# Attention with a sliding window and a GEGLU block: reciprocals through a DRAM tile, q and k by halves, scores half a batch ahead

## The chip, the core and the metric

The kernel runs on one core of a Trainium2 chip. Time is the device time of one execution in microseconds (us). One execution of the kernel before was also profiled; its span is counted from the first to the last recorded event. The engines are called TensorE (PE), VectorE (DVE), ScalarE (ACT), GpSimd (POOL) and SyncE (SP). PEld is TensorE's load of weights; SPq and POOLq are the instruction queues of SyncE and GpSimd, which here issue transfers (DMAs).

## The reference

Eight batches, eight heads, 576 positions, 64 values per head. Each query sees itself and the 127 positions before it, with a bias that falls off linearly with the distance. The heads side by side make rows of 512, 4608 of them, which go through a gated block of width 1536.

```python
scores = scale * np.matmul(q, k.transpose(0, 1, 3, 2))
rel = pos[:, None] - pos[None, :]
mask = (rel >= 0) & (rel < window)
scores = np.where(mask, scores + bias[None], -1000000000.0)
attn = np.exp(scores - max)
attn = attn / (np.sum(attn, axis=-1, keepdims=True) + 1e-09)
x = np.matmul(attn, v)            # to (4608, 512)
out = (gelu(x @ w_gate) * (x @ w_val)) @ w_out
```

## The kernel before

**Attention, batch by batch.** GpSimd loads q and k of a batch (`load_qk`, L75) in slabs of 128 positions by all eight heads and turns them into bf16 on the way: five transfers for q, five for k, the last of 64 positions. There is one slab buffer for q and one for k. The first batch is transposed by TensorE (`transposes`, L110); every other one by SyncE with transposing transfers (`transposes_dma`, L123), five for k and then five for q, each from 128 (or 64) positions by 512 columns into `kT` and `qT`, of which there are two sets, for even and odd batches.

The scores of a batch are eight steps (`scores`, L303): for each pair of heads c the blocks j = 1, 2 (`scores1`), then j = 0, 3 (`scores2`); block 4 of two pairs is done with the first of them (`scores0`). A step is a few matmuls of 64 rows (L135), the exponential on ScalarE (L142) into the tile `P`, and on VectorE the product with a mask that holds window and bias (L145). `P` has three buffers of two pairs each. `sums` (L189) adds up the weights with matmuls against ones, and VectorE takes the reciprocals (L203, L204). They stand in sixteen equal rows for each head and are spread over 64 partitions for each head by 32 copies on SyncE (L212) into the tile `rb`. `values` (L214) multiplies the weights with v for one pair and VectorE multiplies by `rb` (L227), which gives `xT`.

**The gated block, in nine groups of 512 rows.** `gate_val` (L233) makes one of twelve tiles of 128 hidden columns: eight matmuls (L240), gelu on ScalarE (L244), a product on VectorE (L245). `out_half` (L249) is half of one of four output tiles: six matmuls of 512 columns (L255); after the second half the tile is copied to `osb` (L261, or in the last groups L105 and L107 in turn) and SyncE stores it (L265).

**Order.** Each engine works through its instructions in the order of the program; SyncE and GpSimd also issue their transfers in that order, and one that waits holds all that stand behind it. PSUM has eight banks, taken in turn. Before the groups batches 0 and 1 are scored, with values(0) among the scores of batch 1. In group g the loads and transposes of batch g+2 are issued first, then come the twelve gate tiles with the four values of batch g+1 among them (after tiles 4, 6, 8 and 10), then the eight score steps of batch g+2 with an output half behind each of the first seven, then sums(g+2) and the last half. Groups 6 to 8 have no scores.

At the start GpSimd issues q and k of batch 0, makes the constants, and issues v of batch 0, q and k of batch 1, the weights in eight transfers (L97), v of batch 1 and the output weights (L301). The masks of all heads are made at once.

Of the kernel before, what the change touches and what calls it, by code (L numbers as in the profile page):

```python
# [7 lines left out]
FP32 = mybir.dt.float32  # L8
BF16 = mybir.dt.bfloat16
AF = mybir.ActivationFunctionType  # L10
# [14 lines left out]
def kernel(  # L25
# [10 lines left out]
    nc = tc.nc  # L36
# [21 lines left out]
    def bank():  # L58
        return psum.tile([128, 512], FP32, name="ps")
# [12 lines left out]

    slabs = {}

    def load_qk(b):  # L75
        for nm, src in (("qsb", q), ("ksb", k)):
            t = slab.tile([128, 5, DM], BF16, name=nm)
            slabs[nm, b] = t
            for j in range(5):
                sz = min(128, S - 128 * j)  # L80
                nc.gpsimd.dma_start(  # L81
                    out=t[0:sz, j, :].rearrange("p (h d) -> p h d", h=H),
                    in_=src[b][:, 128 * j:128 * j + sz, :].rearrange("h p d -> p h d"),
                )
# [16 lines left out]
    flip = [0]  # L101

    def evac(dst, src):
        if flip[0] % 2 == 0:
            nc.vector.tensor_copy(out=dst, in_=src)  # L105
        else:
            nc.scalar.copy(out=dst, in_=src)  # L107
        flip[0] += 1

    def transposes(b, i):  # L110
        nm, c = (("qsb", "ksb")[i // 4], i % 4)
        src = slabs[nm, b]
        ps = bank().bitcast(BF16)
        for j in range(5):
            sz = min(128, S - 128 * j)
            nc.tensor.transpose(  # L116
                out=ps[:, 128 * j:128 * j + sz],
                in_=src[0:sz, j, 128 * c:128 * (c + 1)],
                identity=ident[0:sz, 0:sz])
        dst = qT[b % 2][:, c, :] if nm == "qsb" else kT[b % 2][:, c, 64:64 + S]  # L120
        evac(dst, ps[:, 0:S])

    def transposes_dma(b):  # L123
        for nm, dst, off in (("ksb", kT[b % 2], 64), ("qsb", qT[b % 2], 0)):
            for j in range(5):
                sz = min(128, S - 128 * j)
                nc.sync.dma_start_transpose(  # L127
                    out=dst[:, :, off + 128 * j:off + 128 * j + sz],
                    in_=slabs[nm, b][0:sz, j, :])

    probs = {}

# [56 lines left out]
    def sums(b):  # L189

        ps = [bank(), bank()]
        for j in range(5):
            for s, a, e, col in pieces(j):
                for i in (0, 1):
                    for c in range(4):
                        nc.tensor.matmul(  # L196
                            out=ps[s][32 * c:32 * c + 32, a - QS * s:e - QS * s],
                            lhsT=ones[:, i, :],
                            rhs=probs[b, c - c % 2][:, c % 2, i, col:col + e - a],
                            start=(i == 0 and j == 2 * s), stop=(i == 1 and j == 2 * s + 2),  # L200
                            skip_group_check=True)
        r = r_pool.tile([128, S], FP32, name="r")
        nc.vector.reciprocal(r[:, 0:QS], ps[0][:, 0:QS])  # L203
        nc.vector.reciprocal(r[:, QS:S], ps[1][:, 0:S - QS])  # L204
        rb = r_pool.tile([128, 4, S], FP32, name="rb")
        recip[b] = rb
        for c in range(4):
            for i in (0, 1):
                row = 32 * c + 16 * i
                for m in range(4):  # L210
                    lo = 64 * i + 16 * m
                    nc.sync.dma_start(out=rb[lo:lo + 16, c, :], in_=r[row:row + 16, :])  # L212

    def values(b, c):  # L214
        P = probs[b, c - c % 2][:, c % 2]
# [33 lines left out]
    def out_half(g, u):  # L249
        t, half = u // 2, u % 2  # L250
        if half == 0:
            acc[g] = bank()
        po = acc[g]
        for f in range(6 * half, 6 * half + 6):
            nc.tensor.matmul(  # L255
                out=po, lhsT=hid[g][:, f, 128 * t:128 * (t + 1)],
                rhs=wo[:, f, :], start=(f == 0), stop=(f == NF - 1))
        if half == 1:
            osb = o_pool.tile([128, DM], FP32, name="osb")
            if g < B - 2:  # L260
                nc.vector.tensor_copy(out=osb, in_=po)  # L261
            else:
                evac(osb, po)
            r0 = 512 * g + 128 * t
            nc.sync.dma_start(out=out[r0:r0 + 128, :], in_=osb)  # L265


    load_qk(0)
    nc.vector.memset(ident, 0.0)
    nc.gpsimd.affine_select(  # L270
        out=ident, in_=ident, compare_op=ALU.not_equal, fill=1.0,
        base=0, pattern=[[-1, 128]], channel_multiplier=1)
    relt = consts.tile([128, 256], mybir.dt.int32, name="relt")
    tmpl = consts.tile([128, 256], FP32, name="tmpl")
    nc.gpsimd.iota(relt, pattern=[[1, 256]], base=0, channel_multiplier=-1)
    nc.gpsimd.tensor_copy(out=tmpl, in_=relt)
    for base, step, chan in ((0, 1, -1), (W - 1, -1, 1)):
        nc.gpsimd.affine_select(
            out=tmpl, in_=tmpl, compare_op=ALU.is_ge, fill=1e9,
            base=base, pattern=[[step, 256]], channel_multiplier=chan)  # L280
    load_v(0)
    for i in range(2):
# [6 lines left out]
    for h in range(H):  # L289
        slope = 2.0 ** (-8.0 * (h + 1) / H)  # L290
        nc.scalar.activation(out=emask[:, h, :], in_=tmpl, func=AF.Exp, scale=-slope)
    nc.vector.tensor_copy(out=emask2[:, :, 0:256], in_=emask)
    nc.vector.memset(emask2[0:64, :, 256:448], 0.0)
    nc.vector.tensor_copy(out=emask2[64:128, :, 256:448], in_=emask[64:128, :, 64:256])
    nc.vector.tensor_copy(out=emask2[:, :, 448:576], in_=emask[:, :, 0:128])
    step = DFF // 4
    load_qk(1)
    for s in range(4):
        load_w(step * s, step * (s + 1))
    load_v(1)  # L300
    nc.gpsimd.dma_start(out=wo, in_=moe_w_out.rearrange("(c p) f -> p c f", p=128))  # L301

    def scores(b):  # L303

        for c in range(4):
            if c % 2 == 0:
                yield lambda c=c: (scores0(b, c), scores1(b, c))
            else:
                yield lambda c=c: scores1(b, c)
            yield lambda c=c: scores2(b, c)  # L310


    for i in (0, 1, 2, 3):
        transposes(0, i)
        transposes(0, 4 + i)
    transposes_dma(1)
    for st in scores(0):
        st()
    sums(0)
    first = list(scores(1))  # L320
    for st in first[0:4]:
        st()
    for c in range(2):
        values(0, c)
    for st in first[4:8]:
        st()
    for c in range(2, 4):
        values(0, c)
    sums(1)

    for g in range(NG):
        if g + 2 < B:
            load_qk(g + 2)
            transposes_dma(g + 2)
        for f in range(NF):
            gate_val(g, f)
            if g + 1 < B and f in (4, 6, 8, 10):
                values(g + 1, f // 2 - 2)  # L340
        b = g + 2
        if b < B:
            load_v(b)
            for u, st in enumerate(scores(b)):
                st()
                if u < 7:
                    out_half(g, u)
            sums(b)
            out_half(g, 7)
        else:  # L350
            for u in range(8):
                out_half(g, u)


# [28 lines left out]
```

## Time and profile before

| | |
|---|---|
| median of three runs | 524.69 us (524.18 to 524.70) |
| the profiled execution | 523.94 us |
| its span | 522.0 us |
| PE busy | 365.5 us (70%) |
| DVE, ACT, POOL busy | 197.8, 164.3, 110.3 us |
| mean granted TensorE clock | 0.895 |
| DMA, mean over the span | 89 GB/s, 46.46 MB |

Matmuls are pipelined, so the durations of neighbours overlap and are not to be added up; differences of their starts are. A row of the timeline merges neighbours of one kind: start, length, engine, line, operation, output and inputs, shape, number, and in brackets the idle time ahead of them with what ended it. On SyncE's queue the length is the time in which the queue was busy with issuing.

### The profile page before, as it was taken

The page shows a single profiled execution, that of the slowest core. Times are in us where ns is not written, and L with a number is a line of the kernel's source. Part 1 is how long each engine was busy: PE and PEld are TensorE (multiplying, and loading weights), DVE is VectorE, ACT ScalarE, POOL GpSimd, SP SyncE. Part 2 cuts the span into 40 slices and gives each one's busy share as a digit, 9 for nine tenths or more (in the row PEclk, how much of TensorE's full clock was granted, in tenths as well). Part 3 has the DMA queues.
Part 4 walks back from the last instruction along what each step waited for, and adds up shares of the span by engine and source line. Part 5 has one row for each costly group of instructions (what it writes and reads, how often), then busy time and mean ns, then how long its engine had stood idle before and what let it go on. Part 6 is the DMA issues. An engine that isn't in the chain of part 4 may idle for free.

```text
span 522.0 us, 6526 instructions
## 1 busy us (share of the span) xinstructions
PE 365.5 (70%) x2384; PEld 164.8 (32%) x2424; DVE 197.8 (38%) x298; ACT 164.3 (31%) x300; POOL 110.3 (21%) x138
## 2 busy tenths in 40 slices
PE   1710629909891689528990889258962999999996
PEld 0410414403440234203440344123420344444442
DVE  0640235414641274305641364226540464233231
ACT  1800602306331352216230542125321532132230
POOL 9952450009000630027000800054000000000000
PEclk9999868958996699959996899869995999999999
DMA  9999995239824992349124982399232112200102
GB/s 90 118 142 190 202 186 62 58 88 128 91 56 100 98 125 55 88 75 175 43 56 108 117 103 57 97 85 146 51 90 61 62 31 53 90 20 21 60 1 81
DMA packets 166192, 46.46 MB, mean 89 GB/s; under 512 B 151824, under 2 KB 157456, under 8 KB 166160
## 3 DMA queue, kind: packets, MB, share of 16 engines
q0 software_dynamic: 118288, 18.88, 48.9%
q1 hardware_dynamic: 47872, 27.16, 20.8%
q8 instruction: 19, 0.31, 0.2%
q14 instruction: 13, 0.11, 0.1%
HBM read 37.75 MB, written 9.44 MB: 90 GB/s over the span
## 4 chain that ended last, share of the span: by engine, by line
PE 46%; SPq 32%; DMA 10%; issue 5%; DVE 3%; POOL 2%; ACT 1%; DVEq 0%; POOLq 0%
PE ps L240 20%; PE ps L255 19%; SPq L127 16%; SPq L212 15%; DMA qT<-qsb 5%; PE ps L135 4%; DMA rb<-r 4%; DMA ksb<-in_k_dram 2%; POOL qsb L81 2%; PE ps L221 1%; DVE r L204 1%; PE ps L196 1%; DVE P L145 1%; PE ps L116 1%; ACT P L142 1%
## 5 line engine op out<-in xcount | busy, mean ns | idle before, releaser
L142 ACT ACTIVATE P<-ps 128x512 bf16<-128x512 f32 (+2 forms) x160 | 73.4, 555 | 146.8 <-PE ps L135 146.8
L240 PE MATMUL ps<-xT,wg 128*128 128x512 bf16 x414 | 111.6, 383 | 7.0 <-DVE xT L227 5.7
L244 ACT ACTIVATE gelu<-ps 128x512 bf16<-128x512 f32 x108 | 64.5, 597 | 164.4 <-PE ps L240 161.5
L135 PE MATMUL ps<-qT,kT 64*128 64x256 bf16 (+2 forms) x320 | 33.1, 301 | 113.9 <-DMA qT<-qsb 112.0
L240 PE MATMUL ps<-xT,wv 128*128 128x512 bf16 x431 | 111.9, 382 | 0.1
L255 PE MATMUL ps<-wo,hT 128*128 128x512 bf16 x411 | 107.8, 405 | 3.8 <-issue 2.6
L245 DVE TENSOR_TENSOR hT<-ps,gelu 128x512 bf16<-128x512 f32 x108 | 74.2, 688 | 81.5 <-PE ps L240 81.4
L145 DVE TENSOR_TENSOR P<-P,emask 128x1024 bf16<-128x1024 bf16 x64 | 46.1, 725 | 152.1 <-ACT P L142 152.1
L81 POOL DMA_DIRECT2D qsb<-in_q_dram x40 | 33.7, 866 | 225.6 <-DMA qT<-qsb 224.4
L240 PEld LDWEIGHTS <-wv 128*128 128x128 bf16 x432 | 42.6, 99 | 57.5 <-DMA vb<-in_v_dram 5.5
L255 PEld LDWEIGHTS <-hT 128*128 128x128 bf16 x432 | 40.3, 103 | 56.9 <-issue 19.7
L135 PEld LDWEIGHTS <-kT 64*128 64x128 bf16 x320 | 12.6, 103 | 142.0 <-issue 141.4
L240 PEld LDWEIGHTS <-wg 128*128 128x128 bf16 x432 | 40.1, 98 | 50.1 <-issue 2.4
L227 DVE TENSOR_TENSOR xT<-ps,rb 128x320 bf16<-128x320 f32 x64 | 26.2, 452 | 47.0 <-DMA rb<-r 41.8
L90 POOL DMA_DIRECT2D vb<-in_v_dram x40 | 34.5, 923 | 12.0 <-DMA wg<-in_moe_w_gate_dram 6.0
L81 POOL DMA_DIRECT2D ksb<-in_k_dram x40 | 33.9, 901 | 7.6 <-DMA wo<-in_moe_w_out_dram 6.4
L196 PE MATMUL ps<-P,ones 128*32 128x128 bf16 (+2 forms) x384 | 13.4, 270 | 16.6 <-DVE P L145 16.6
L221 PE MATMUL ps<-P,vb 128*64 128x128 bf16 (+2 forms) x384 | 22.2, 256 | 0.0
L221 PEld LDWEIGHTS <-vb 128*64 128x64 bf16 x384 | 15.6, 115 | 12.6 <-issue 12.6
L203 DVE RECIPROCAL r<-ps 128x320 f32<-128x320 f32 x8 | 17.3, 2157 | 5.7 <-PE ps L196 5.7
L261 DVE COPY osb<-ps 128x512 f32<-128x512 f32 x24 | 16.1, 671 | 0.9 <-PE ps L255 0.8
L196 PEld LDWEIGHTS <-ones 128*32 128x32 bf16 x384 | 10.0, 107 | 20.2 <-issue 19.8
(33 smaller groups left out, 70.3 us busy)
## 6 DMA issues: line engine op xcount, KB each, us to landing
rb<-r SPq DMA_DIRECT2D x256, 36.0 KB, 2.0
out_dram<-osb SPq DMA_DIRECT2D x36, 256.0 KB, 2.2
qsb<-in_q_dram POOLq DMA_DIRECT2D x32, 128.0 KB, 4.1
ksb<-in_k_dram POOLq DMA_DIRECT2D x32, 128.0 KB, 5.2
vb<-in_v_dram POOLq DMA_DIRECT2D x32, 128.0 KB, 5.5
wg<-in_moe_w_gate_dram POOLq DMA_DIRECT2D x4, 384.0 KB, 15.2
wv<-in_moe_w_val_dram POOLq DMA_DIRECT2D x4, 384.0 KB, 17.1
wo<-in_moe_w_out_dram POOLq DMA_DIRECT2D x1, 1536.0 KB, 20.1
```

Source lines behind the costliest of these rows:

```text
L81: nc.gpsimd.dma_start(out=t[0:sz, j, :].rearrange("p (h d) -> p h d", h=H), in_=src[b][:, 128 * j:128 * j + sz, :].rearrange("h p d -> p h ...
L90: nc.gpsimd.dma_start(out=t[lo:128, j, :].rearrange("p (h d) -> p h d", h=H), in_=v[b][:, 128 * j - 64 + lo:128 * j + 64, :].rearrange("h ...
L127: nc.sync.dma_start_transpose(out=dst[:, :, off + 128 * j:off + 128 * j + sz], in_=slabs[nm, b][0:sz, j, :])
L135: nc.tensor.matmul(out=ps[:, col:col + NQ[j]], lhsT=kT[b % 2][lo:lo + 64, c, 128 * j:128 * j + 128], rhs=qT[b % 2][lo:lo + 64, c, Q0[j]:Q0 ...
L142: nc.scalar.activation(out=dst, in_=src, func=AF.Exp, scale=0.125)
L145: nc.vector.tensor_tensor(out=dst, in0=dst, in1=m, op=ALU.mult)
L212: nc.sync.dma_start(out=rb[lo:lo + 16, c, :], in_=r[row:row + 16, :])
L221: nc.tensor.matmul(out=ps[s][64 * i:64 * i + 64, a - QS * s:e - QS * s], lhsT=vb[b % 2][:, j, 64 * h:64 * h + 64], rhs=P[:, i, col:col + e ...
L240: nc.tensor.matmul(out=ps, lhsT=w[:, c, 128 * f:128 * (f + 1)], rhs=xT[:, c, t0:t0 + 512], start=(c == 0), stop=(c == 3))
L244: nc.scalar.activation(out=gl, in_=pg, func=AF.Gelu)
L245: nc.vector.tensor_tensor(out=hid[g][:, f, :], in0=pv, in1=gl, op=ALU.mult)
L255: nc.tensor.matmul(out=po, lhsT=hid[g][:, f, 128 * t:128 * (t + 1)], rhs=wo[:, f, :], start=(f == 0), stop=(f == NF - 1))
```

## The change

1. **Reciprocals.** Instead of 32 copies from SBUF to SBUF, SyncE writes eight rows (one for each head) to a DRAM tile, and then reads them back twice, each time spread over 64 partitions. The second and third transfer wait for the first to land.
2. **Halves of four heads.** q and k are loaded by halves u = 0, 1 of four heads (256 columns); each slab tile is half as wide and has two buffers. The transposing transfers are by halves too: twenty for a batch instead of ten, of 128 (or 64) positions by 256 columns. TensorE's transposes of batch 0 go pair by pair, and VectorE alone copies them out.
3. **Order.** A list `todo` holds the score steps of all batches. Ahead of group 0 stand batch 0 and half of batch 1, with the masks of each pair made just before its first step. Group 0 takes eight steps (the rest of batch 1 and half of batch 2), group 1 twelve (to the end of batch 3), groups 2 to 5 eight each. In groups 0 and 1 the values of the next batch stand behind the score steps (two of them in the midst in group 1), in the others after gate tiles 5, 7, 9 and 11. The first output half follows the second score step, no longer the first.
4. All output tiles are copied by ScalarE.
5. At the start GpSimd issues both halves of batch 0 and half of batch 1, v(0), the weights, the other half of batch 1, the output weights, v(1). In the groups v(g+2) is issued with q and k.

```diff
-    slab = ctx.enter_context(tc.tile_pool(name="slab", bufs=1))
+    slab = ctx.enter_context(tc.tile_pool(name="slab", bufs=2))
+    d_pool = ctx.enter_context(
+        tc.tile_pool(name="dp", bufs=2, space=bass.MemoryType.DRAM))
...
-    def load_qk(b):
+    def load_qk(b, u):
...
-            t = slab.tile([128, 5, DM], BF16, name=nm)
+            t = slab.tile([128, 5, DM // 2], BF16, name=nm)
...
-                    in_=src[b][:, 128 * j:128 * j + sz, :].rearrange("h p d -> p h d"),
+                    in_=src[b][4 * u:4 * u + 4, 128 * j:128 * j + sz, :].rearrange("h p d -> p h d"),
...
-    def transposes_dma(b):
+    def transposes_dma(b, u):
...
-                    out=dst[:, :, off + 128 * j:off + 128 * j + sz],
-                    in_=slabs[nm, b][0:sz, j, :])
+                    out=dst[:, 2 * u:2 * u + 2, off + 128 * j:off + 128 * j + sz],
+                    in_=slabs[nm, b, u][0:sz, j, :])
...
-        for c in range(4):
-            for i in (0, 1):
-                row = 32 * c + 16 * i
-                for m in range(4):
-                    lo = 64 * i + 16 * m
-                    nc.sync.dma_start(out=rb[lo:lo + 16, c, :], in_=r[row:row + 16, :])
+        d = d_pool.tile([4, 2, S], FP32, name="rd")
+        nc.sync.dma_start(out=d.rearrange("c i s -> (c i) s"), in_=r[0:128:16, :])
+        for i in (0, 1):
+            nc.sync.dma_start(
+                out=rb[64 * i:64 * i + 64, :, :],
+                in_=d[:, i, :].unsqueeze(0).to_broadcast((64, 4, S)))
...
-            if g < B - 2:
-                nc.vector.tensor_copy(out=osb, in_=po)
-            else:
-                evac(osb, po)
+            nc.scalar.copy(out=osb, in_=po)
...
+    transposes(0, 0)
+    transposes(0, 1)
+    for c in range(4):
+        masks(c)
+        todo.pop(0)[1]()
+        if c + 2 < 4:
+            transposes(0, c + 2)
+        todo.pop(0)[1]()
+    transposes_dma(1, 0)
     sums(0)
...
+    for n in range(4):
+        todo.pop(0)[1]()
+    for c in range(4):
         values(0, c)
...
+    LOADS = {0: ((1, 1), (2, 0)), 1: ((2, 1), (3, 0), (3, 1))}
     for g in range(NG):
+        late = g < 2
+        for b, u in LOADS.get(g, ((g + 2, 0), (g + 2, 1))):
+            if b < B:
+                if (b, u) != (1, 1):
+                    load_qk(b, u)
+                transposes_dma(b, u)
         if g + 2 < B:
-            load_qk(g + 2)
-            transposes_dma(g + 2)
+            load_v(g + 2)
         for f in range(NF):
             gate_val(g, f)
-            if g + 1 < B and f in (4, 6, 8, 10):
-                values(g + 1, f // 2 - 2)
...
+            if g >= 2 and g + 1 < B and f in (5, 7, 9, 11):
+                values(g + 1, (f - 5) // 2)
+        n = min(len(todo), 12 if g == 1 else 8)
+        halves = 0
+        for m in range(n):
+            b, st = todo.pop(0)
+            st()
+            if b == g + 1 and len(todo) % 8 == 0:
+                sums(b)
+            if (m + 1) * 7 // n > halves:
+                out_half(g, halves)
+                halves += 1
+            if g == 1 and m == 7:
+                values(2, 0)
+                values(2, 1)
+        if late:
+            for c in range(2 if g else 0, 4):
+                values(g + 1, c)
+        if n and g >= 1 and g + 2 < B:
+            sums(g + 2)
+        for u in range(halves, 8):
+            out_half(g, u)
```

How the instructions stand on two engines, line, operation, tiles and shape; x4 means four in a row. SyncE, from the stores of group 1 to the transposes of batch 4 that group 2 issues, before (`kT_91` and `qT_89` are the set for even batches):

```order
L265 DMA out_dram<-osb 128x512 x3
L212 DMA rb<-r 16x576 x32
L265 DMA out_dram<-osb 128x512
L127 DMA_TRANSPOSE kT_91<-ksb 128x4x128 x4
L127 DMA_TRANSPOSE kT_91<-ksb 128x4x64
L127 DMA_TRANSPOSE qT_89<-qsb 128x4x128 x4
L127 DMA_TRANSPOSE qT_89<-qsb 128x4x64
```

The same place in a later group of the changed kernel (group 3's stores, then the first half of the transposes of batch 6, which group 4 issues; `kT_93` and `qT_91` are the set for even batches there):

```order
L257 DMA out_dram<-osb 128x512 x3
L203 DMA rd<-r 8x576
L205 DMA rb<-rd 64x4x576 x2
L257 DMA out_dram<-osb 128x512
L122 DMA_TRANSPOSE kT_93<-ksb 128x2x128 x4
L122 DMA_TRANSPOSE kT_93<-ksb 128x2x64
L122 DMA_TRANSPOSE qT_91<-qsb 128x2x128 x4
L122 DMA_TRANSPOSE qT_91<-qsb 128x2x64
```

The 32 copies have become three transfers; the four rows of transposes are half as wide (2 blocks of 128 columns instead of 4) and come twice, once for each half.

SyncE in group 1 of the changed kernel, from the end of the second half of batch 2 over both halves of batch 3 to the reciprocals of batch 2 (tile numbers shown, since the two halves would read alike):

```order
L122 DMA_TRANSPOSE qT0_91<-qsb_999 128x2x64
L122 DMA_TRANSPOSE kT1_94<-ksb_1027 128x2x128 x4
L122 DMA_TRANSPOSE kT1_94<-ksb_1027 128x2x64
L122 DMA_TRANSPOSE qT1_92<-qsb_1021 128x2x128 x4
L122 DMA_TRANSPOSE qT1_92<-qsb_1021 128x2x64
L122 DMA_TRANSPOSE kT1_94<-ksb_1049 128x2x128 x4
L122 DMA_TRANSPOSE kT1_94<-ksb_1049 128x2x64
L122 DMA_TRANSPOSE qT1_92<-qsb_1043 128x2x128 x4
L122 DMA_TRANSPOSE qT1_92<-qsb_1043 128x2x64
L203 DMA rd_1333<-r_1329 8x576
L205 DMA rb_1332<-rd_1333 64x4x576 x2
L257 DMA out_0_dram<-osb_1343 128x512
```

All thirty transposes of group 1 stand ahead of the reciprocals of batch 2 and of the group's stores; before, group 1 had ten transposes, and no reciprocals of batch 2 in it.

GpSimd at the start, before, from v of batch 0 to the first of the weights (`vb_93` is v's tile for even batches):

```order
L90 DMA vb_93<-in_v_dram 128x8x64 x4
L81 DMA qsb<-in_q_dram 128x8x64 x4
L81 DMA qsb<-in_q_dram 64x8x64
L81 DMA ksb<-in_k_dram 128x8x64 x4
L81 DMA ksb<-in_k_dram 64x8x64
L97 DMA wg<-in_moe_w_gate_dram 128x4x384
```

And in the changed kernel, from the last of the weights on (`vb_96` is v's tile for odd batches):

```order
L100 DMA wv<-in_moe_w_val_dram 128x4x384
L84 DMA qsb<-in_q_dram 128x4x64 x4
L84 DMA qsb<-in_q_dram 64x4x64
L84 DMA ksb<-in_k_dram 128x4x64 x4
L84 DMA ksb<-in_k_dram 64x4x64
L280 DMA wo<-in_moe_w_out_dram 128x12x512
L93 DMA vb_96<-in_v_dram 64x8x64
```

Before, the whole of batch 1 stands ahead of the weights; now its first half stands ahead of v and the weights, and its second half, shown here, behind them.

More of the change, by code (lines that the diff above doesn't have):

```diff
@@ L99, in load_w, with transposes @@
                 in_=src[:, lo:hi].rearrange("(c p) f -> p c f", p=128))
[L101 to L105, printed above, removed]
-        else:
[L107 to L121, printed above, removed]
-    def transposes_dma(b):
+    def transposes(b, c):
+        for nm in ("qsb", "ksb"):
+            src = slabs[nm, b, c // 2]
+            ps = bank().bitcast(BF16)
+            lo = 128 * (c % 2)
+            for j in range(5):
+                sz = min(128, S - 128 * j)
+                nc.tensor.transpose(
+                    out=ps[:, 128 * j:128 * j + sz],
+                    in_=src[0:sz, j, lo:lo + 128],
+                    identity=ident[0:sz, 0:sz])
+            dst = qT[b % 2][:, c, :] if nm == "qsb" else kT[b % 2][:, c, 64:64 + S]
+            nc.vector.tensor_copy(out=dst, in_=ps[:, 0:S])
+    def transposes_dma(b, u):
         for nm, dst, off in (("ksb", kT[b % 2], 64), ("qsb", qT[b % 2], 0)):
@@ L280 @@
             base=base, pattern=[[step, 256]], channel_multiplier=chan)
+    load_qk(0, 1)
+    load_qk(1, 0)
     load_v(0)
+    step = DFF // 4
+    for n in range(4):
+        load_w(step * n, step * (n + 1))
+    load_qk(1, 1)
+    nc.gpsimd.dma_start(out=wo, in_=moe_w_out.rearrange("(c p) f -> p c f", p=128))
+    load_v(1)
     for i in range(2):
@@ L296 @@
[L296 to L315, printed above, removed]
@@ L316, with masks @@
-    transposes_dma(1)
-    for st in scores(0):
-        st()
+    def masks(c):
+        for h in (2 * c, 2 * c + 1):
+            slope = 2.0 ** (-8.0 * (h + 1) / H)
+            nc.scalar.activation(out=emask[:, h, :], in_=tmpl, func=AF.Exp, scale=-slope)
+        e, e2 = emask[:, 2 * c:2 * c + 2, :], emask2[:, 2 * c:2 * c + 2, :]
+        nc.vector.tensor_copy(out=e2[:, :, 0:256], in_=e)
+        nc.vector.tensor_copy(out=e2[64:128, :, 256:448], in_=e[64:128, :, 64:256])
+        nc.vector.tensor_copy(out=e2[:, :, 448:576], in_=e[:, :, 0:128])
@@ new lines, in steps @@
+    def steps():
+        for b in range(B):
+            for c in range(4):
+                if c % 2 == 0:
+                    yield b, lambda b=b, c=c: (scores0(b, c), scores1(b, c))
+                else:
+                    yield b, lambda b=b, c=c: scores1(b, c)
+                yield b, lambda b=b, c=c: scores2(b, c)
+    todo = list(steps())
+    transposes(0, 0)
[6 more added lines that the diff above has]
+        todo.pop(0)[1]()
@@ L319 @@
+    transposes_dma(1, 0)
     sums(0)
[L320 to L323, printed above, removed]
+    for n in range(4):
+        todo.pop(0)[1]()
+    for c in range(4):
         values(0, c)
[L325 to L329, printed above, removed]
-    for g in range(NG):
+    LOADS = {0: ((1, 1), (2, 0)), 1: ((2, 1), (3, 0), (3, 1))}
+    for g in range(NG):
+        late = g < 2
[4 more added lines that the diff above has]
+                transposes_dma(b, u)
```

29 lines of the change are left out of this document (5 added, 24 removed).

## The prediction

> **What bounds the kernel now.** I read the table of waits first, then TensorE's and SyncE's rows in the timeline beside one another, over one group and over the start. From the table of waits (waiting engine and line, releaser: us in total, times, longest):
>
> ```profile
> PE ps L135 <- DMA qT<-qsb: 112.0, 7, 25.9
> ```
>
> TensorE is busy for 365.5 of 522.0 us by the page; of its idle time, 112 us are seven waits of the scores (L135) for transposed q, the last tile of a batch to be transposed. The timeline (start us, us, engine, line, operation) of TensorE in group 1, then of SyncE's queue there:
>
> ```profile
> 173.61 0.82 PE L135 MATMUL ps<-qT,kT 64*128 64x128 bf16 x8 [14.40 <-DMA qT<-qsb]
> 174.37 2.74 PE L255 MATMUL ps<-wo,hT 128*128 128x512 bf16 x6
> ...
> 181.10 0.37 PE L135 MATMUL ps<-qT,kT 64*128 64x192 bf16 x4
> 181.40 1.47 PE L255 MATMUL ps<-wo,hT 128*128 128x512 bf16 x6
> 182.80 0.50 PE L135 MATMUL ps<-qT,kT 64*128 64x128 bf16 x8
> ...
> 192.62 1.03 PE L240 MATMUL ps<-xT,wg 128*128 128x512 bf16 x4
> ```
> ```profile
> 137.69 20.88 SPq L212 DMA_DIRECT2D rb<-r  x32
> ...
> 159.31 6.47 SPq L127 DMA_TRANSPOSE kT<-ksb  x5
> 165.83 6.47 SPq L127 DMA_TRANSPOSE qT<-qsb  x5
> ```
>
> SyncE issues in order: 32 small copies of the reciprocals take 20.9 us, and only then come the ten transposes, 13.0 us, for which the scores wait. Group 6 begins here:
>
> ```profile
> 420.91 1.03 PE L240 MATMUL ps<-xT,wg 128*128 128x512 bf16 x4
> ```
>
> Call S(g) the first gate matmul of group g. S(2) is 192.6 and S(6) 420.9, so a group takes 57.07 us, and from S(6) to the end are 522.0 - 420.9 = 101.1. The stall is 14.4. Behind it the clock is low: 173.61 to 181.10 is 7.49 us for three pairs of a score step and an output half, where the next pair takes 1.70 (182.80 - 181.10; 0.14 more for the pair that opens a half batch): 5.24, so 2.25 are lost. A group without the stall is 57.07 - 14.40 - 2.25 = **40.4 us**, of which 23.7 come before the scores (57.07 - 14.40 - 19.01, the last from 173.61 to 192.62).
>
> The start, on SyncE, on TensorE, and a landing from the chain of work:
>
> ```profile
> 25.33 9.18 SPq L127 DMA_TRANSPOSE kT<-ksb  x5
> 34.55 13.76 SPq L127 DMA_TRANSPOSE qT<-qsb  x5
> 48.40 24.21 SPq L212 DMA_DIRECT2D rb<-r  x32
> ```
> ```profile
> 55.76 2.16 PE L135 MATMUL ps<-qT,kT 64*128 64x128 bf16 x20 [25.89 <-DMA qT<-qsb]
> ...
> 78.40 0.59 PE L240 MATMUL ps<-xT,wg 128*128 128x512 bf16 x1 [5.25 <-DVE xT L227]
> ```
> ```profile
> 45.31 10.32 DMA qT<-qsb
> ```
>
> Here the ten transposes take 22.9 us, beside the weights, and the last needs 10.3 us to land; batch 1's scores wait for it and group 0 waits for the last copies: S(0) = 78.4.
>
> **The change part by part.**
>
> *The reciprocals.* 32 issues, 20.9 us of SyncE per batch, go. Three come: one to DRAM, and two broadcasts of 590 KB that wait for its landing. Nearest rows for the first, SyncE's issue of the output and its landing (last number):
>
> ```profile
> L265 SPq DMA_DIRECT2D out_dram<-osb x36: 332/333/529, 123.4 to 518.6; - x36
> ```
> ```profile
> out_dram<-osb SPq DMA_DIRECT2D x36, 256.0 KB, 2.2
> ```
>
> So 2.2 us until SyncE may go on, and 0.65 for each broadcast (20.88/32). The broadcasts' landing is in no row: between 2.2 us (256 KB above) and 20.9 us (the same bytes in 32 issues). The output's bytes and rows are nearest; at twice its size I take 4.5.
>
> *The transposes.* Twenty of 256 columns replace ten of 512. SyncE's price, from the rows of L127 between 103 and 117 us (min/median/max ns):
>
> ```profile
> L127 SPq DMA_TRANSPOSE kT<-ksb x5: 1196/1200/1217, 103.0 to 108.3; - x5
> ...
> DMA to landing us min/median/max: 2.3/2.3/2.4
> ```
>
> One of these five has 64 rows, half the data, and costs no less. So I take 1.30 (13.0/10) for a half too; the other end is 0.65, if width counts where height doesn't. [...]
>
> *A steady group (2 to 5).* SyncE's queue: the reciprocals are ready 2.1 us behind S (193.05 + 1.70 - 192.62, from VectorE's rows; L227 below is the multiply by them, two instructions for each pair of heads, 0.82 us together):
>
> ```profile
> 189.47 0.76 DVE L145 TENSOR_TENSOR P<-P,emask 128x1152 bf16<-128x1152 bf16 x1 [0.90 <-ACT P L142]
> 190.98 2.16 DVE L203 RECIPROCAL r<-ps 128x320 f32<-128x320 f32 x1 [0.75 <-PE ps L196]
> 193.05 1.70 DVE L204 RECIPROCAL r<-ps 128x256 f32<-128x256 f32 x1
> ```
> ```profile
> L227 DVE TENSOR_TENSOR xT<-ps,rb 128x320 bf16<-128x320 f32 x64 | 26.2, 452 | 47.0 <-DMA rb<-r 41.8
> ```
>
> SyncE waits 2.2 for the landing in DRAM, and behind that wait stand the broadcasts (1.3), the last output (0.4) and the twenty transposes, for which TensorE waits: they begin at S + 6.0. The first ten have landed at 6.0 + 9 x 1.3 + 2.3 = 20, before the scores at 23.7. The last ten land at 6.0 + 19 x 1.3 + 2.3 = 33.0, while the fifth score step is due at 23.7 + 5.6 = 29.3 by TensorE's pairs. It waits 3.7 us; this is what takes the place of the 14.4. What follows it took 9.8 before (182.80 to 192.62); one output half more (1.4) lies behind it now, and it covers about 0.7 of the old wait for the masks: 10.5. The group takes **43.5**. The broadcasts land at S + 10, when values first need them (six gate tiles, 10.4): hidden. Loads of q and k, now 20 issues on GpSimd, start as soon as the same half of the batch before is transposed, most of a group ahead, with v between them: hidden, unless they slow the transposes (rival three).
>
> *The output copies move to ScalarE.* Its rows of half a batch's exps (with a table load), and a copy's mean:
>
> ```profile
> 183.12 1.64 ACT L142 ACTIVATE P<-ps 128x256 bf16<-128x256 f32 x4 [0.64 <-PE ps L135]
> 185.04 0.98 ACT L142 ACTIVATE P<-ps 128x448 bf16<-128x448 f32 x2 [0.28 <-PE ps L135]
> 186.76 1.08 ACT L142 ACTIVATE P<-ps 128x512 bf16<-128x512 f32 x2 [0.75 <-PE ps L135]
> 188.46 0.98 ACT L142 ACTIVATE P<-ps 128x448 bf16<-128x448 f32 x2 [0.61 <-PE ps L135]
> 189.46 1.28 ACT L244 ACT_TABLE_LOAD   x1
> ```
> ```profile
> L107 ACT COPY osb<-ps 128x512 f32<-128x512 f32 x6 | 3.5, 586 | 31.0 <-PE ps L255 25.5 <-DMA out_dram<-osb 5.4
> ```
>
> Two of these half batches are 9.4, three copies 1.8, the table load 1.3 (no stall hides it now), the last gelu ahead of it under 1; from the last mask to S took 3.2 (189.47 to 192.62). That is 16.7 at most, against TensorE's own 16.7 (40.4 - 23.7): I book nothing, but this cover is used up, and whatever ScalarE takes beyond it would be on the path, one for one.
>
> *The start.* GpSimd's price for a load is known for 64 and 128 rows, about 0.7 and 0.9, so a half of 512 runs is put at 0.7:
>
> ```profile
> L81 POOL DMA_DIRECT2D ksb<-in_k_dram x40: 690/934/958, 5.5 to 352.7; - x40
> ```
>
> Some 25 of them and 2 us of constants bring the k half of batch 1 to its landing at about 25, as before. Its ten transposes take 13 (steady price) to 23 us (start); with half the data 19, nearer to the start's row since the weights come beside them: 44. They land by 53 (2.3 to 10.3 behind). The masks, now made two heads at a time, and VectorE's sole copying of the first transposes stand beside these loads and cost nothing, since batch 1's scores come 25 us later. The reciprocals to DRAM stand behind the transposes and land then too; the broadcasts at 62, beside weights still arriving (8 us, above the quiet 4.5), four pairs of multiplies 4 x 0.82: **S(0) = 65**, 58 to 72, against 78.4.
>
> *Group 0.* Its gates have no values between them, so 23.7 less some 3, and 2 of low clock: 22.8. Half a batch of scores up to the sums of batch 1 takes 9.2 (table load, exps, a copy and the last gelu 7.5, then mask and sums). The values of batch 1, at the end of this group now, need what the gates hid before: reciprocals 3.5, DRAM 2.2, broadcasts 5.5, multiplies 3.3, together 14.5, longer than the four pairs and values that TensorE has left. **46.5**.
>
> *Group 1.* Thirty transposes stand in one row and the reciprocals of batch 2 behind them: the last output 1.1, then 30 x 1.3, is 40.1; DRAM 2.2 and broadcasts 5.2 more, so values(2) get them at S + 47.5, while TensorE could use them at about 34. Four of its eight PSUM banks hold those values, the next output half finds none free, and VectorE stands before the masks behind. The rest (three score steps, three output halves, values, sums, the last half) is 9: **56.5**.
>
> Sum: 65 + 46.5 + 56.5 + 4 x 43.5 + 101.1 = 443.1; the profiled execution had 523.94 for a span of 522.0, and the median, 524.69, is 0.75 above it: 443.1 + 1.9 + 0.75 = **445.7 us**. With an issue price c the four places give 308 + 106 c.
>
> **The rivals.**
> 1. *A half costs half* (c of 0.65 to 0.9). Transposes land in time, groups 2 to 5 take 40.4, group 1 about 51.3, S(0) 63: 63 + 46.5 + 51.3 + 161.6 + 101.1 + 2.7 = 426. For it: the bytes per instruction are halved. Against: the 64-row transpose, which has half of them too. TensorE would then be the bound but for the start and group 1.
> 2. *The broadcasts land late*, at 12 us instead of 4.5: 64 readers of the same rows of DRAM. Steady groups hide it behind the transposes; the start, groups 0 and 1 do not: + 4 + 7 + 7, 464. For it: landings at the start, for 36 KB:
>
> ```profile
> DMA to landing us min/median/max: 4.7/5.4/7.5
> ```
>
> 3. *Transposes slow beside loads*, the side of slower. Loads of the next batch are now issued as soon as a half is transposed, so beside the other half's. At the start transposes beside loads cost 2.3 us; 308 + 106 x 2.3 = 552. It decides at c = 2.04. The DMA share (last but one number) at the start and in the quiet transposes:
>
> ```profile
> 25.00:48.00 23.00, 2.29 (x46) 1.80 (x45) 6.03 (x6) 2.05 (x5) 10.45 (x14) 1.00 1.47 161
> 159.00:172.00 13.00, 0.21 (x1) 0.00 (x0) 1.42 (x3) 1.28 (x1) 0.00 (x0) 0.59 0.45 109
> ```
>
> Against it: loads take GpSimd some 20 x 0.7 = 14 us per group, which cannot cover 26 us of transposes, and no weights come any more.
>
> **The numbers.** Forecast 0.53 (430 to 460), half price 0.28 (414 to 434), late broadcasts 0.10, transposes at 1.5 to 2.0 0.05, slower 0.03, 0.01 no change. The range of 414 to 462 leaves out the last cases and a part of the third. 0.2%, 1 us, is about what can be told from no change: faster 0.96, same 0.01, slower 0.03.
>
> **What would show it.** SyncE's row of twenty transposes in a steady group: 26 us or 13; a wait of 3 to 4 us for qT or kT in the middle of the scores of groups 2 to 5, or none; S(0) between 58 and 72; group 1 the longest, with VectorE waiting for rb. It is wrong if S(0) stays near 78, if steady groups stay above 50, or if another engine than SyncE ends the last wait there.

## The result and the profile after

| | before | changed |
|---|---|---|
| median | 524.70 us (4 runs) | **456.35 us** (456.32 to 456.53, 4 runs) |
| ratio to before | | 0.8699, 95% interval 0.8684 to 0.8714 |
| profiled span | 522.0 us | 454.6 us |
| mean granted TensorE clock | 0.895 | 0.935 |
| S(0), S(1), S(2), S(6) | 78.4, 135.5, 192.6, 420.9 | 56.7, 109.4, 170.3, 354.3 |

S(g) is, as in the prediction, the first matmul of the gates of group g (from the timeline). Only S(0) of the kernel before is not quite that: two single gate matmuls stand at 71.7 and 72.8 already, and 78.4 is the one behind the last wait. The kernel is 13% faster; the forecast was 445.7 with 414 to 462. Against its sum in spans, 443.1, the profiled execution has 11.5 us more: the start took 8.3 us less than forecast, group 0 took 6.2 more, group 1 4.4 more, groups 2 to 5 together 10.0 more, and the rest 0.8 less. That the total lies so near is in part luck: misses of 20.6 us one way met 9.1 us the other way.

**The steady groups.** The table of waits of the changed kernel has TensorE's wait for transposed q at 42.6 us where 112.0 stood, in eight pieces:

```profile
PE ps L130 <- DMA qT<-qsb: 42.6, 8, 11.2
```

The timeline of TensorE in group 3 (S(3) = 215.0, S(4) = 262.0) shows where the piece lies now:

```profile
242.66 1.47 PE L250 MATMUL ps<-wo,hT 128*128 128x512 bf16 x6
249.15 0.82 PE L130 MATMUL ps<-qT,kT 64*128 64x128 bf16 x8 [5.02 <-DMA qT<-qsb]
249.90 2.74 PE L250 MATMUL ps<-wo,hT 128*128 128x512 bf16 x6
252.58 0.55 PE L130 MATMUL ps<-qT,kT 64*128 64x192 bf16 x4
253.06 2.53 PE L250 MATMUL ps<-wo,hT 128*128 128x512 bf16 x6
```

Three output halves are done, the first half of the batch is scored, and the fifth score step waits 5.0 us for the second half of qT. SyncE's queue in the same group:

```profile
217.18 0.62 SPq L203 DMA_DIRECT2D rd<-r  x1
219.04 1.26 SPq L205 DMA_DIRECT2D rb<-rd  x2
220.39 0.55 SPq L257 DMA_DIRECT2D out_dram<-osb  x1
221.05 6.49 SPq L122 DMA_TRANSPOSE kT<-ksb  x5
227.59 6.38 SPq L122 DMA_TRANSPOSE qT<-qsb  x5
234.08 7.39 SPq L122 DMA_TRANSPOSE kT<-ksb  x5
241.52 6.38 SPq L122 DMA_TRANSPOSE qT<-qsb  x5
```

The reciprocals go out at S + 2.2, the transposes begin at S + 6.0 (221.05 - 215.03), and the twenty end at S + 32.9: 26.9 us, 1.34 each. The price of one, in ns, min/median/max over all 70 of k, each half as wide as before:

```profile
L122 SPq DMA_TRANSPOSE kT<-ksb x70: 1167/1195/1897, 24.2 to 332.8; - x70
```

The median of the wide ones before was 1211. Half the width saves 1% of the median.

**The start.** TensorE's wait for the transposes of batch 1 and the first gates, then SyncE:

```profile
44.12 2.16 PE L130 MATMUL ps<-qT,kT 64*128 64x128 bf16 x20 [11.21 <-DMA qT<-qsb]
...
56.70 2.77 PE L235 MATMUL ps<-xT,wg 128*128 128x512 bf16 x4 [7.35 <-DVE xT L222]
```
```profile
24.23 6.45 SPq L122 DMA_TRANSPOSE kT<-ksb  x5
30.72 7.76 SPq L122 DMA_TRANSPOSE qT<-qsb  x5
38.58 0.70 SPq L203 DMA_DIRECT2D rd<-r  x1
44.19 1.32 SPq L205 DMA_DIRECT2D rb<-rd  x2
```

Ten transposes take 14.3 us here, hardly more than in a steady group (12.9 and 13.8 in group 3), though the weights, issued from 29.0 to 35.2 us, come beside them; then DRAM 5.6 us, and group 0 waits for the multiplies behind the broadcasts. Ten of full width took 22.9 us at this place in the kernel before; in the run recip_only below the last three of the ten took 7.2 (41.88 to 49.09). In the run halves, which issues the weights in the order of the kernel before (where the weights, the output weights last, are under way from 25.2 to 68.3 us), ten half-wide ones take 12.8 us:

```profile
43.64 6.34 SPq L131 DMA_TRANSPOSE kT<-ksb  x5
50.03 6.38 SPq L131 DMA_TRANSPOSE qT<-qsb  x5
```

So beside the weights the width counted (22.9 us against 14.3 and 12.8 for ten), where in the quiet it hardly did (1211 ns against 1195). What holds SyncE there is not shown.

**Groups 0 and 1.** In group 0 the scores of batch 2 wait; SyncE begins its transposes at 81.4, and GpSimd had stood before its loads until the output weights had landed:

```profile
97.01 0.82 PE L130 MATMUL ps<-qT,kT 64*128 64x128 bf16 x8 [6.61 <-DMA qT<-qsb]
```
```profile
73.41 0.75 POOL L84 DMA_DIRECT2D qsb<-in_q_dram  x1 [7.85 <-DMA wo<-in_moe_w_out_dram]
```

In group 1 the reciprocals of batch 2 leave SyncE at 150.4, behind thirty transposes (S(1) = 109.4, so S + 41.0, where 40.1 was forecast). VectorE waits for what they are spread into:

```profile
162.22 1.55 DVE L222 TENSOR_TENSOR xT<-ps,rb 128x320 bf16<-128x320 f32 x4 [13.94 <-DMA rb<-rd]
```

and the landing of the broadcasts, min/median/max in us, is longer than the 4.5 that I took. The trace has it for one of the two in five of the eight batches, not for batch 2; there the first multiply stands 9.7 us behind the issue (152.57 to 162.22):

```profile
DMA to landing us min/median/max: 5.4/6.0/8.2
```

### The profile page after: what moved, and what is told of

The parts are those of the page before. It is cut to its first block, busy times and chain, and to the rows that moved or that the text cites. A ratio compares the mean times of both kernels' runs of the same rounds, so it can differ in the third digit from the quotient of the medians.

```text
span 454.6 us, 6481 instructions
## 1 busy us (share of the span) xinstructions
PE 368.8 (81%) x2424; PEld 167.0 (37%) x2424; DVE 184.4 (41%) x281; ACT 176.3 (39%) x326; POOL 157.6 (35%) x218
## 5 line engine op out<-in xcount | busy, mean ns | idle before, releaser
L250 PE MATMUL ps<-wo,hT 128*128 128x512 bf16 x432 | 115.1, 416 | 0.1
L84 POOL DMA_DIRECT2D qsb<-in_q_dram x80 | 58.0, 754 | 131.5 <-DMA qT<-qsb 113.2
L130 PE MATMUL ps<-qT,kT 64*128 64x256 bf16 (+2 forms) x320 | 29.6, 304 | 45.4 <-DMA qT<-qsb 42.6
L84 POOL DMA_DIRECT2D ksb<-in_k_dram x80 | 58.3, 781 | 18.4 <-DMA qsb<-in_q_dram 9.3
L235 PEld LDWEIGHTS <-wg 128*128 128x128 bf16 x432 | 41.1, 98 | 58.1 <-issue 8.9
L250 PEld LDWEIGHTS <-hT 128*128 128x128 bf16 x432 | 41.3, 104 | 57.4 <-issue 22.5
L255 ACT COPY osb<-ps 128x512 f32<-128x512 f32 x36 | 21.2, 588 | 69.8 <-PE ps L250 52.4
L130 PEld LDWEIGHTS <-kT 64*128 64x128 bf16 x320 | 12.9, 105 | 68.2 <-issue 56.5
L191 PE MATMUL ps<-P,ones 128*32 128x128 bf16 (+2 forms) x384 | 14.5, 281 | 13.9 <-DVE P L140 13.7
L216 PE MATMUL ps<-P,vb 128*64 128x128 bf16 (+2 forms) x384 | 20.8, 248 | 1.4 <-DVE xT L222 1.4
## 6 DMA issues: line engine op xcount, KB each, us to landing
wg<-in_moe_w_gate_dram POOLq DMA_DIRECT2D x4, 384.0 KB, 12.9
wv<-in_moe_w_val_dram POOLq DMA_DIRECT2D x4, 384.0 KB, 14.3
wo<-in_moe_w_out_dram POOLq DMA_DIRECT2D x1, 1536.0 KB, 14.3
```

The lines of the kernel that those rows point to most:

```text
L84: nc.gpsimd.dma_start(out=t[0:sz, j, :].rearrange("p (h d) -> p h d", h=H // 2), in_=src[b][4 * u:4 * u + 4, 128 * j:128 * j + sz, :].rear ...
L130: nc.tensor.matmul(out=ps[:, col:col + NQ[j]], lhsT=kT[b % 2][lo:lo + 64, c, 128 * j:128 * j + 128], rhs=qT[b % 2][lo:lo + 64, c, Q0[j]:Q0 ...
L191: nc.tensor.matmul(out=ps[s][32 * c:32 * c + 32, a - QS * s:e - QS * s], lhsT=ones[:, i, :], rhs=probs[b, c - c % 2][:, c % 2, i, col:col ...
L216: nc.tensor.matmul(out=ps[s][64 * i:64 * i + 64, a - QS * s:e - QS * s], lhsT=vb[b % 2][:, j, 64 * h:64 * h + 64], rhs=P[:, i, col:col + e ...
L235: nc.tensor.matmul(out=ps, lhsT=w[:, c, 128 * f:128 * (f + 1)], rhs=xT[:, c, t0:t0 + 512], start=(c == 0), stop=(c == 3))
L250: nc.tensor.matmul(out=po, lhsT=hid[g][:, f, 128 * t:128 * (t + 1)], rhs=wo[:, f, :], start=(f == 0), stop=(f == NF - 1))
```

## The experiments

Nine further kernels were run, each timed beside the kernel before. The theory: SyncE's queue decides, by the number of its instructions; the three reciprocal transfers bring the gain, and the halves take a part of it back. The rivals: the price of a transpose goes with its width; or halves and order carry the gain. The table has all of them (S from each profile; the ratio is to the kernel before, timed beside it, with its 95% interval).

| run | median us | ratio | S(0) | S(2) | S(6) | span | groups 2 to 5, mean |
|---|---|---|---|---|---|---|---|
| before | 524.7 | 1 | 78.4 | 192.6 | 420.9 | 522.0 | 57.1 |
| changed | 456.35 | 0.870 (0.868 to 0.871) | 56.7 | 170.3 | 354.3 | 454.6 | 46.0 |
| wide | 430.57 | 0.818 (0.814 to 0.822) | 55.7 | 171.0 | 329.3 | 429.1 | 39.6 |
| recip_only | 419.95 | 0.799 (0.794 to 0.803) | 74.5 | 156.8 | 318.3 | 418.5 | 40.4 |
| no_recip | 542.36 | 1.030 (1.025 to 1.036) | | 183.0 | 441.3 | 541.5 | 64.6 |
| start | 455.42 | 0.866 (0.861 to 0.870) | 56.4 | 171.2 | 354.0 | 454.2 | 45.7 |
| halves | 462.53 | 0.878 (0.875 to 0.882) | 82.0 | 176.8 | 358.3 | 458.5 | 45.4 |
| copies | 420.72 | 0.801 (0.797 to 0.805) | 73.9 | 156.1 | 317.7 | 417.8 | 40.4 |
| wide2 | 427.31 | 0.812 (0.809 to 0.815) | 54.7 | 167.5 | 325.2 | 425.2 | 39.4 |
| te1 | 405.07 | 0.771 (0.767 to 0.774) | 56.5 | 142.5 | 304.0 | 403.8 | 40.4 |
| te2 | 397.06 | 0.754 (0.751 to 0.757) | 56.5 | 139.9 | 295.3 | 395.1 | 38.9 |

### wide: full-width transposes from batch 4 on

```diff
+        if 2 <= g < B - 2:
+            load_wide(g + 2)
+            transposes_wide(g + 2)
-        for b, u in LOADS.get(g, ((g + 2, 0), (g + 2, 1))):
+        for b, u in LOADS.get(g, ()):
```

`load_wide` issues the same twenty half loads into one slab of 512 columns, `transposes_wide` the ten transposes of the kernel before.

> The changed kernel, but from batch 4 on the transposes are of full width again (ten of 512 columns from a slab of one buffer, loaded by the same half loads). Theory: SyncE pays about 1.3 us for a transpose whatever its width; the ten then end by about S + 20, the wait in the midst of the scores of groups 2 to 5 (4.0 to 5.5 us, and the low clock behind it) goes, each of these groups falls from 46.0 to about 40.6 us, and the time from 456 to about 435 us. Rival, price goes with width: ten wide transposes occupy SyncE as long as twenty halves, 26 us, the groups stay at 46 us, or grow since no half is ready early, and the time stays at 456 us or above.

430.57 us, and the groups fall to 39.6: the theory's side, by somewhat more than it said. Within this one run, with no weights beside them, SyncE's prices for wide transposes (two rows, groups 2 to 5) and for halves (the third, group 1) can be compared:

```profile
L94 SPq DMA_TRANSPOSE qT<-qw x20: 1245/1264/2075, 185.8 to 311.1; - x20
L94 SPq DMA_TRANSPOSE kT<-kw x19: 1187/1302/2423, 179.3 to 304.1; - x19
```
```profile
L143 SPq DMA_TRANSPOSE kT<-ksb x15: 1168/1193/1226, 111.2 to 143.5; - x15
```

Twice the width costs 6 to 9% more of SyncE's time, not 100%. And the wait in the middle of the scores is gone; what is left, at their beginning, is 0.8 us:

```profile
234.41 0.71 PE L151 MATMUL ps<-qT,kT 64*128 64x128 bf16 x12 [0.83 <-DMA qT<-qw]
```

### recip_only: the reciprocals alone

The kernel before with the three transfers in `sums` and the pool for `rd`, nothing else.

> The kernel before with the reciprocals through a DRAM tile in three transfers and nothing else. Theory: the 32 copies ahead of the transposes were the whole of the steady wait (14.4 us and 2.3 of low clock); without them the ten transposes land at about S + 20, ahead of the scores, each of six groups takes about 40.6 us, the first group begins at about 72 instead of 78.4, and the time is about 419 us, below the changed kernel. Rival, the halves and the order carry a good part of the gain: more than 456 us.

419.95 us: the reciprocals alone beat the whole change by 36 us. TensorE and SyncE in group 2 (S(2) = 156.8, scores from 180.4):

```profile
180.42 0.50 PE L137 MATMUL ps<-qT,kT 64*128 64x128 bf16 x8
```
```profile
158.98 0.62 SPq L210 DMA_DIRECT2D rd<-r  x1
160.79 1.28 SPq L212 DMA_DIRECT2D rb<-rd  x2
162.17 0.55 SPq L267 DMA_DIRECT2D out_dram<-osb  x1
162.83 8.11 SPq L129 DMA_TRANSPOSE kT<-ksb  x5
170.99 6.48 SPq L129 DMA_TRANSPOSE qT<-qsb  x5
```

No idle time stands ahead of the scores; SyncE is through 2.9 us before they begin (177.5), and each group takes the 40.4 us that the prediction named as the group without its stall.

### no_recip: the change without its reciprocals

```diff
-        d = d_pool.tile([4, 2, S], FP32, name="rd")
...
+        for c in range(4):
+            for i in (0, 1):
...
+                    nc.sync.dma_start(out=rb[lo:lo + 16, c, :], in_=r[row:row + 16, :])
```

> The changed kernel with the 32 copies of the reciprocals in place of the three transfers; halves and order stay. Theory: SyncE is then busy 20.9 + 26.8 us ahead of the second half of a batch, groups 2 to 5 take about 65 us instead of 46, groups 0 and 1 and the start some 10 us each more, about 565 us, slower than the kernel before. Rival, halves and order give most of the gain by themselves: below 480 us.

542.36 us, slower than the kernel before; 23 us less than expected. S(2) is 12.6 us later than in the changed kernel, where some 30 were expected for the start and groups 0 and 1 together, but the groups 2 to 5 come out at 64.6 for the expected 65. (S(0) has no entry: the first gate matmuls wait one by one, from 50.8 to 67.1.) SyncE and TensorE in group 3:

```profile
254.69 21.19 SPq L205 DMA_DIRECT2D rb<-r  x32
275.98 0.53 SPq L255 DMA_DIRECT2D out_dram<-osb  x1
276.64 6.79 SPq L120 DMA_TRANSPOSE kT<-ksb  x5
283.48 6.38 SPq L120 DMA_TRANSPOSE qT<-qsb  x5
289.96 6.33 SPq L120 DMA_TRANSPOSE kT<-ksb  x5
296.34 6.39 SPq L120 DMA_TRANSPOSE qT<-qsb  x5
```
```profile
291.11 1.20 PE L128 MATMUL ps<-qT,kT 64*128 64x128 bf16 x12 [15.01 <-DMA qT<-qsb]
304.00 0.82 PE L128 MATMUL ps<-qT,kT 64*128 64x128 bf16 x8 [4.81 <-DMA qT<-qsb]
```

Now both halves are late. That rules out the rival by which halves and order carry the gain.

### halves: recip_only with halves, order as before

`load_qk`, the slab pool and `transposes_dma` as in the change; batch 0 and 1 loaded as (0,0), (0,1), (1,0), (1,1); in group g both halves of batch g+2 are loaded and transposed in turn.

> The kernel before with the reciprocals through DRAM (the run recip_only, 419.95 us) and the halves of four heads in loads, slabs and transposes; the order of the work as before. Theory: twenty transposes at 1.3 us put the second half at S + 34, so a wait comes back in the midst of the scores, a group takes about 46 us instead of 40.4, and the start loses some 10 us to ten more transposes beside the weights: 455 to 465 us. Rival, the loss of the changed kernel against recip_only lies in the order of the first groups and not in the halves: at most 425 us.

462.53 us, as expected. So the halves by themselves cost 43 us against recip_only: 5.0 us in each of groups 2 to 5 (45.4 against 40.4), 7.5 at the start, and 5.7 and 6.8 in groups 0 and 1 (S(1) is 129.6 here and 116.4 there). The wait in the middle of the scores is the same as in the changed kernel (group 3; the operation's place in the batch is the fifth step):

```profile
257.19 0.82 PE L139 MATMUL ps<-qT,kT 64*128 64x128 bf16 x8 [4.16 <-DMA qT<-qsb]
```

### copies: recip_only with all output copies on ScalarE

```diff
-            if g < B - 2:
-                nc.vector.tensor_copy(out=osb, in_=po)
-            else:
-                evac(osb, po)
+            nc.scalar.copy(out=osb, in_=po)
```

> recip_only with all output copies on ScalarE. Theory: ScalarE has 12 to 13 us of work in a score stage of 16.7, so the copies are hidden and the time stays within 2 us of 419.95. Rival, ScalarE is now the bound of the score stage, since the output half that could cover the last exponentials is not there in this order: some 1 to 2 us for each of six groups, 426 to 432 us.

420.72 us, and the same 40.4 us for a group: the intervals of this ratio and of recip_only's overlap, so there is no difference that can be told.

### start: batch 2 ahead of the output weights

```diff
+    load_qk(2, 0)
     nc.gpsimd.dma_start(out=wo, in_=moe_w_out.rearrange("(c p) f -> p c f", p=128))
...
-                if (b, u) != (1, 1):
+                if (b, u) not in ((1, 1), (2, 0)):
```

> The changed kernel, but the loads of the first half of batch 2 are issued ahead of the output weights, not behind them and v of batch 1. Theory: group 0's wait of 6.6 us for qT of batch 2 comes from these loads, which GpSimd could issue only when the output weights had landed; the transposes follow those of batch 1 at about 73 instead of 81 us and the wait goes, but the reciprocals of batch 1 then set the end, so group 1 begins 3 to 5 us earlier and the time is 451 to 454 us. Rival, the queue of SyncE sets the end of group 0 anyway: 456 us, no difference.

455.42 us; the ratios of this run and of the changed kernel overlap, so there is no difference that can be told. The theory had the mechanism and not the gain: the wait of 6.6 us for qT is gone, and S(1) is 109.1 instead of 109.4, since VectorE now waits for the broadcasts of batch 1:

```profile
105.45 3.01 DVE L222 TENSOR_TENSOR xT<-ps,rb 128x320 bf16<-128x320 f32 x8 [6.04 <-DMA rb<-rd]
```

They were issued at 95.7 and 96.3, and the first multiply stands at 105.4, beside loads of v and q. Two chains of nearly the same length end group 0; to shorten one gives nothing.

### wide2: full width from batch 2 on, other loads at the start

The edit against the run wide:

```diff
     load_qk(1, 0)
+    load_qk(1, 1)
     load_v(0)
...
-    load_qk(1, 1)
+    load_wide(2)
     nc.gpsimd.dma_start(out=wo, in_=moe_w_out.rearrange("(c p) f -> p c f", p=128))
...
-        for b, u in LOADS.get(g, ()):
...
+        if g == 0:
+            transposes_dma(1, 1)
+        if g < B - 2:
+            if g > 0:
+                load_wide(g + 2)
+            transposes_wide(g + 2)
```

> The run wide, with full width from batch 2 on, the second half of batch 1 loaded ahead of v and the weights and batch 2 ahead of the output weights. Theory: group 1 is long (61 us) because thirty transposes stand ahead of the reciprocals of batch 2 and beside them; with ten it falls to about 44 us; group 0 stays near 52, since the values of batch 1 wait for the broadcasts at its end; 411 to 416 us. Rival, group 1 is long because of the broadcasts' landing and its twelve steps: it stays above 52 us and the time above 420.

427.31 us: missed by 11 us. Group 1 fell from 61.0 (run wide) to 49.4 us, so ten transposes in place of thirty take 11.6 us off it, more than half of what it has above the 40.4 of recip_only; the rival's bound of 52 does not hold for it, nor do the theory's 44. But group 0 grew from 54.2 to 63.4, because the first output half now waits for the output weights that stand behind batch 2:

```profile
90.73 0.61 PE L271 MATMUL ps<-wo,hT 128*128 128x512 bf16 x1 [10.49 <-DMA wo<-in_moe_w_out_dram]
```

### te1 and te2: two versions that beat both

te1 is recip_only with batch 1 transposed by TensorE:

```diff
-    transposes_dma(1)
     for st in scores(0):
         st()
     sums(0)
+    for i in (0, 1, 2, 3):
+        transposes(1, i)
+        transposes(1, 4 + i)
```

> recip_only with batch 1 transposed by TensorE at the start, like batch 0. Theory: what then sets the first group is SyncE's ten transposes beside the weights, which land at 55 us; without them batch 1 is scored from about 36 us on, the reciprocals of batch 0 go out at about 36 us, and group 0 begins at 56 to 60 instead of 74.5: 402 to 408 us. Rival, the broadcasts beside the weights set the start: group 0 begins at 68 us or later and the time is above 413 us.

405.07 us; group 0 begins at 56.5. Once batch 0 is transposed, TensorE's longest wait at the start is the one for the multiplies behind the broadcasts of batch 0:

```profile
50.55 0.34 PE L198 MATMUL ps<-P,ones 128*32 128x192 bf16 x2 [6.60 <-DVE xT L229]
```

te2 moves the output halves by one step, as the change has them:

```diff
-                if u < 7:
-                    out_half(g, u)
+                if u > 0:
+                    out_half(g, u - 1)
```

> The run te1 with the first output half behind the second score step instead of the first, so that one stands between the last score step and the sums, as in the changed kernel. Theory: this half covers about 1.2 us of TensorE's wait for the last masks (1.66 us in each group of te1, 0.46 in the changed kernel), six groups make 5 to 7 us: 398 to 400 us. Rival, the first two steps without a half between them now wait for ScalarE's exponentials and PSUM banks and give it back: 403 us or more.

397.06 us: 1.5 us for each group (38.9), a little more than expected. TensorE's waits for the masks ahead of the sums, in all:

```profile
PE ps L198 <- DVE P L147: 7.9, 10, 2.0
```

They were 16.2 in te1.

## Why the prediction was right, point by point

1. **The reciprocals**: right as the source of the gain (recip_only, no_recip). The landing in DRAM took 1.9 us in the steady group shown (217.18 to 219.04) for the 2.2 taken. The broadcasts' landing was mis-sized: 6.0 us in the median where the trace has it, for 4.5; and from the issue of the first to the multiply that waits for both it took 11.6 us at the start (44.19 to 55.83), 9.8 in group 0 of the run start and 9.7 in group 1. The second rival, 12 us, was nearer there than the 4.5; it had the chance 0.10.
2. **"So I take 1.30 for a half too"**: right, 1.34 in the group shown. The row on which it stood, a transpose of 64 rows that cost as much as one of 128 (1196 to 1217 ns for five, one of them of 64 rows), held for the width as well, where no weights come beside it: 1193 ns against 1264 and 1302 in one run. The first rival, half price, falls for the groups by the runs wide and halves; beside the weights it was near the mark (12.8 us for ten against 22.9). Its 51.3 us for group 1 is not worked out there: by the prediction's own terms, values at S + 34 or 35 and 9 behind them, it would be 43 to 45.
3. **"The group takes 43.5"**: the place of the new wait, the fifth score step, and its cause were right; the term was mis-sized by 2.5 us. Two things: the waits were 4.0, 5.0, 5.5 and 4.5 us for 3.7; and the step "what follows it took 9.8 before" failed: from the end of the wait to the next S it was 11.6, 12.9, 11.4 and 12.7 us, where 10.5 was booked. The 9.8 lie behind three pairs in which the clock had recovered (0.67 over the pairs, 173.6 to 181.1, and 1.00 behind them). Behind the new wait it is low again:

```profile
249.20:262.00 12.80, 12.34 (x98) 4.76 (x99) 4.54 (x5) 5.66 (x12) 11.38 (x15) 0.76 1.26 126
```

   The granted clock (third number from the end) is 0.76 in the 12.8 us from the wait to S(4), and two output halves take 2.74 and 2.53 us for 1.47. In the other three groups the clock behind the wait is 0.85, 0.87 and 0.77. I had booked this loss for the stall that goes and forgotten it for the one that comes.
4. **The output copies on ScalarE**: nothing, right (copies). That a half behind the last score step covers the masks' wait was right as well, and worth more than the 0.7 booked: 0.46 us of that wait are left in each of the changed kernel's groups 2 to 5, where recip_only has 1.66, and te2 gained 1.5 us a group by it.
5. **S(0) = 65**: 56.7, outside my bounds of 58 to 72. "Nearer to the start's row since the weights come beside them" failed: ten halves took 14.3 us, not 19. Landing and DRAM took 5.6 for 9. The broadcasts took 11.6 to the first multiply for 9, which is longer than assumed; but the first gates stand 0.9 behind the first multiply (55.83 to 56.70), where 3.3 for all four pairs was booked.
6. **Group 0, 46.5**: 52.7. It left out that batch 2's loads stand behind the output weights in GpSimd's queue; the run start shows that without this wait the broadcasts end the group at the same time. There the path of the sum can be followed: the broadcasts take 9.8 us to the first multiply for 5.5 booked, 4.3 of the 6.2 us that are missing.
7. **Group 1, 56.5**: 60.9. Its mechanism was right (thirty transposes ahead of the reciprocals; wide2 takes 11.6 us off it with ten); the missing 4.4 us are about the broadcasts' longer way, 9.7 for 5.2.
8. **The rival of slow transposes beside loads**, which would have made the kernel slower: no. In the group shown the first ten, without loads, took 12.9 us and the second ten 13.8.

What the prediction did not ask is what each part would be worth alone. By the starts of the groups, against recip_only the whole change gains 17.8 us at the start, and loses 10.7 in group 0 (52.7 against 42.0), 20.5 in group 1 (60.9 against 40.4) and 22.5 in groups 2 to 5. The halves alone bring 20.0 of the 22.5 (run halves), and 5.7 and 6.8 of the loss in groups 0 and 1. The other 5.0 and 13.7 there came with the new order; that they come from the half batch ahead, which puts values and broadcasts at the end of a group where no gate covers them, is argued from the waits shown and not tested by itself. Whether some other order of the loads would save the half batch ahead stays open; start and wide2 each moved the wait elsewhere.

## What to carry to other kernels

Where a queue that issues transfers is late, count its instructions ahead of the transfer that is waited for: in the groups here their number decided (0.65 us for a copy of 36 KB, 0.63 for a broadcast of 590 KB), so merging 32 into 3 paid (57.1 to 40.4 us a group in recip_only) and cutting ten transposes into twenty cost (40.4 to 45.4 in halves), though the bytes stayed the same. Beside heavy loads measure anew: there ten wide transposes took 22.9 us (13.0 in a group), and ten half-wide ones 14.3 and 12.8. Judge the parts of a change one by one against the same wait: here one part was worth more than all together. And where a sum leaves a new wait on TensorE, book the low clock behind it as well: here waits of 4.0 to 5.5 us had 0.76 to 0.87 behind them.

## What the runs showed of the hardware that was not expected

- SyncE's price for a transposing transfer hardly depended on its width where no weights come beside it: 1193 ns for 128 x 256, 1264 to 1302 for 128 x 512, in one run; nor on its rows: 1168 to 1226 ns for fifteen of 256 columns there, three of them of 64 rows. Beside the weights, ten of 512 columns took 22.9 us, ten of 256 columns 14.3 and 12.8.
- Of two broadcasts from the same 18 KB of DRAM, 590 KB each, one took 5.4 to 8.2 us to land (in the five batches for which the trace has it), and the multiply that waited for both stood 9.7 to 11.6 us behind the first issue; an output store of 256 KB took 2.7 us to land in the median.
- Waits of 4.0 to 5.5 us on TensorE were followed by a granted clock of 0.76 to 0.87 over the 11.4 to 12.8 us up to the next group.
